# Cluster similarities by float32 matmuls on four column tiles, with the prologue in another order

## The chip, the cores and the metric

The kernel runs on one NeuronCore of a Trainium2 chip. TensorE multiplies matrices and writes to PSUM, VectorE and ScalarE compute and read PSUM, GpSimd computes beside them, and the queue of SyncE (SP) issues most DMA transfers. The metric is the device time of one execution in microseconds, lower is better.

## What is computed

Three layers follow each other: attention within clusters, a mixture of experts that sends every token to one expert, and a last layer. The change lies in the first. Queries and keys get a cluster each, the centroid with the largest cosine similarity; a query sees only the keys of its own cluster.

```python
B, H, S, D = q.shape            # 2, 8, 768, 64; 16 centroids for each head
c_n = centroids / (norm(centroids) + 1e-06)
q_assign = argmax(einsum('bhsd,hcd->bhsc', q_n, c_n))     # k_assign likewise
mask = q_assign[:, :, :, None] == k_assign[:, :, None, :]
scores = where(mask, scale * q @ k.T, -1e9)
attn = softmax(scores)
x = attn @ v                    # then the experts and the last layer
```

The norm of a query or key does not change which centroid is nearest, so the kernel normalises the centroids alone. Two centroids can be close, so the similarities are wanted to float32 accuracy.

## The kernel before

**Stages.** The attention works on eight pairs of heads (two batches, four pairs each). For a pair, `load_qk` brings queries and keys, by dimension (two heads of 64 on 128 partitions, 768 tokens), into the tile `raw`, of which there are two. `a_hi` (L589, ScalarE) rounds them to fp32r, the reduced float32 of the fast matmul, into the tile `w`, and `a_lo` (L595, GpSimd or VectorE) subtracts that from `raw`: the low part. `a_sims` (L610, L613) multiplies tokens by centroids: for every 128 tokens, the high part by the centroids' high and low parts (64 columns: two halves, two heads, 16 clusters), and the low part by the centroids' high part (32 columns). The tokens are the stationary operand, so the result has them on partitions. `a_sims_red` (L620, VectorE) adds the two halves from PSUM into the tile `sim`. `a_argmax` (L653 to L660, VectorE, three steps) makes one-hot rows `ohb`. `a_moves` (L626, SP) copies parts of `w` between partitions by seven DMAs. `a_aux` (L669, L672, L676, L677) turns the one-hot rows by matmul into auxiliary rows of `w`, which carry the mask into the scores' product, by DMA; `a_aux_first` (L685 to L692) does so for the first head of all without DMA, writing straight into `w`.

**The loop.** `x_max` (L751, L753) and `x_max_halves` (L764, L765, L766) take row maxima of masked scores; `x_row` (L773, L774) turns them into another row of `w`. Then a unit is 128 keys of a head: scores (L799, L800) into one of two PSUM tiles, which `x_max_halves` shares, exponentials (L809, ScalarE), their low parts (L823), and the product with the values (L838 to L840) four units later. `v_scale` (L715 to L729) finds a power of two that scales the values.

**Order.** The program order of each engine is the order in which the code issues, and engines wait for each other by semaphores. The prologue runs a list of names, `PRO`, for the first two pairs; each `warm` in it issues as many idle matmuls (L1188) as the next entry of `WARMS` says. Then, during pair p's twelve units, the work of pair p + 2 (names `hi`, `lo`, `sims`, `red`, `moves`, `arg`, `aux`) is issued at the places that `AT` and `AT_PAIR` give in units. `sims0` and `sims1` (queries, keys) are issued in thirds there, with `b` and `c` for the second and third. `load_qk` of pair p + 3 is issued when pair p begins; that of pair 2 is `lqk2` in `PRO`.

Of the kernel before, what the change touches and what calls it, by code (L numbers as in the profile page):

```python
# [28 lines left out]
# places of the windows, by rising load; the first NF32 use plain float32 products  # L29
CAPS = [128, 176, 192, 200, 208, 224, 240, 320]  # L30
# the first window has its expert picked early, and plain float32 products
CAP0 = CAPS[0]
W0_ROWS = [(t, min(128, CAP0 - 128 * t)) for t in range((CAP0 + 127) // 128)]
# query tiles of the last pair that go (and are gated) first
W0_AT = [3,5]
QT = 3
# chunks of an expert's matrices whose low parts are made by GpSimd
# [12 lines left out]
# the places of the operations beside the pairs' products  # L50
# [69 lines left out]
        'sims0b': 2.0003,  # L120
        'sims0c': 2.0006,
        'sims1b': 4.0003,
        'sims1c': 4.233,
# [45 lines left out]
                   'sims0b': 2.4163,  # L169
                   'sims0c': 2.4166,  # L170
                   'sims1b': 5.5923,
                   'sims1c': 5.5926,
# [38 lines left out]
                   'sims0b': 2.5753000000000004,  # L211
                   'sims0c': 2.702,
                   'sims1b': 4.356,
# [27 lines left out]
                   'sims0b': 2.9203,  # L241
                   'sims0c': 2.952,
                   'sims1b': 4.21,
# [3 lines left out]
                   'row00': 9.523,  # L247
                   'sims1c': 5.27},
# [21 lines left out]
                   'sims0b': 2.9203,  # L270
                   'sims0c': 2.9206,
                   'logb': 8.103299999999999,
                   'acc': 8.554,
                   'sims1b': 4.21,
                   'row00': 9.523,
                   'sims1c': 5.27,
# [19 lines left out]
                   'sims0b': 2.7293000000000003,  # L296
                   'sims0c': 2.7296,
# [3 lines left out]
                   'sims1b': 4.21,  # L301
                   'row00': 9.523,
                   'row01': 10.291,
                   'sims1c': 5.27,
# [22 lines left out]
                   'sims0b': 2.126,  # L327
                   'sims0c': 2.7426,
# [4 lines left out]
                   'sims1b': 4.21,  # L333
                   'sims1c': 5.27,
# [26 lines left out]
                   'sims1b': 3.0163,  # L361
                   'sims1c': 3.0166,
# [28 lines left out]
 'WARMS': [8, 8, 0, 7, 0, 9, 4, 3, 4, 3, 0, 0, 0, 0, 0, 0, 0, 0, 0, 0, 0, 0, 0],  # L391
# [14 lines left out]
def body(ctx, tc, i, o):  # L406
# [21 lines left out]

    qT, kT, v = i["qT"], i["kT"], i["v"]

# [1 line left out]
    def load_qk(p, which=(0, 1)):  # L432
        b, hp = PAIRS[p]
        if "raw" not in st[p]:
# [163 lines left out]
    def a_sims(p, qk, t0=0, t1=NT):  # L598
# [5 lines left out]
        if t0 == 0:  # L604
            s["px", qk] = ps_x.tile([128, 512], F32, tag="px", name=f"psim_{p}_{qk}")
# [1265 lines left out]
```

## Time and profile before

| | |
|---|---|
| runs shown | 657.06, 657.48, 664.31 us; median 657.48 |
| span of the profiled execution | 653.1 us |
| TensorE matmuls | 595.3 us busy, 91% of the span, 4814 instructions |
| VectorE | 477.0 us, 73% |
| ScalarE | 318.4 us, 49% |
| GpSimd | 334.3 us, 51% |
| mean granted clock of TensorE | 0.937 of full speed |

The profile has no other time of the profiled execution than its span, from the first to the last instruction. The attention takes it up to 284 us, then come the gating, the experts (303 to 519 us) and the last layer. Busy time of an engine is a sum over its instructions; what it means in a stretch is read from that stretch.

### The profile page before, as it was taken

To read this page: it belongs to the slowest core of one execution; us is meant where nothing else is said; L and a number is where in the kernel's file an instruction comes from. 1 tells how busy PE (TensorE), PEld (TensorE's weight loads), DVE (VectorE), ACT (ScalarE), POOL (GpSimd) and SP (SyncE) were. 2 spreads that over 40 slices of the span, in tenths; PEclk is the share of its full clock that TensorE was granted. 3 is DMA by queue.
4 is the path that set the end of the run, shared out by engine and by line. 5 is a ranking of instruction groups with operands and counts; after the bars stand their busy time and mean duration, and the time that the engine had idled before them with its cause. 6 is when DMAs were issued, how large, how long until landed. Compare 5 with 4: busy or idle time off the path is not lost. (4 is left out here: it accounts for less than half of the span.)

```text
span 653.1 us, 12986 instructions
## 1 busy us (share of the span) xinstructions
PE 595.3 (91%) x4814; PEld 519.0 (79%) x4814; DVE 477.0 (73%) x860; ACT 318.4 (49%) x684; POOL 334.3 (51%) x341
## 2 busy tenths in 40 slices
PE   7989899999899999969898789898799999999996
PEld 4578788888787888859798788786699778888884
DVE  5856788778677877844779999999978766446540
ACT  3334546455445465521576766664566543323230
POOL 6064747455456667532366756767841663333321
PEclk8957899889788999988999999998899999999999
DMA  6853626253612201075477757676670000000001
GB/s 204 223 151 86 181 83 181 84 166 99 185 40 62 51 30 61 24 287 207 159 252 248 248 206 280 225 254 186 153 192 1 3 16 18 16 33 17 32 17 48
DMA packets 28215, 81.80 MB, mean 125 GB/s; under 512 B 4699, under 2 KB 4971, under 8 KB 28146
## 3 DMA queue, kind: packets, MB, share of 16 engines
q1 hardware_dynamic: 22690, 69.30, 34.7%
q0 software_dynamic: 2352, 6.32, 2.6%
q10 hardware_dynamic: 3104, 5.28, 2.5%
q8 instruction: 41, 0.67, 0.4%
q14 instruction: 28, 0.23, 0.1%
HBM read 55.24 MB, written 11.55 MB: 102 GB/s over the span
## 5 line engine op out<-in xcount | busy, mean ns | idle before, releaser
L823 POOL TENSOR_TENSOR pl<-pe 128x768 f16<-128x768 f32 (+1 forms) x90 | 127.3, 1420 | 95.7 <-ACT pe L809 95.5
L1394 POOL TENSOR_TENSOR wk<-rw,wk 128x512 fp32r<-128x512 f32 x67 | 98.6, 1483 | 72.3 <-ACT wk L1393 59.3
L809 ACT ACTIVATE pe<-pS 128x384 f32<-128x384 f32 x192 | 85.1, 488 | 80.2 <-PE pS L800 72.6
L753 DVE TENSOR_REDUCE ohb<-pm 128x1 bf16<-128x768 f32 x84 | 80.1, 954 | 39.8 <-PE pm L751 38.8
L799 PE MATMUL pS<-w 81*128 81x384 f32 x192 | 79.3, 413 | 1.4 <-DVE mh L765 1.3
L1477 PE MATMUL po<-h,wk 128*128 128x352 f32 (+5 forms) x192 | 62.5, 377 | 17.6 <-DVE h L1506 15.4
L800 PE MATMUL pS<-w 128*128 128x384 f32 x192 | 70.1, 365 | 0.0
L838 PE MATMUL pa<-v,pe 128*128 128x65 f16 x576 | 67.2, 200 | 0.0
L1393 ACT ACTIVATE wk<-rw 128x512 fp32r<-128x512 f32 x112 | 65.6, 625 | 2.0 <-DMA rw<-in_w_dram 1.0
L839 PE MATMUL pa<-v,pe 128*128 128x64 f16 x576 | 66.3, 200 | 0.0
L840 PE MATMUL pa<-v,pl 128*128 128x65 f16 x576 | 66.1, 198 | 0.0
L838 PEld LDWEIGHTS <-pe 128*128 128x128 bf16 x576 | 55.2, 102 | 11.1 <-issue 8.5
L1477 PE MATMUL ph<-xTm,wk 128*128 128x352 f32 (+5 forms) x192 | 62.5, 379 | 1.4 <-DVE xTm L1454 1.3
L751 PE MATMUL pm<-w 80*128 80x512 f32 (+1 forms) x168 | 49.5, 379 | 7.5 <-DVE ohb L753 4.5
L839 PEld LDWEIGHTS <-pe 128*128 128x128 bf16 x576 | 55.9, 102 | 0.0
L840 PEld LDWEIGHTS <-pl 128*128 128x128 f16 x576 | 55.8, 102 | 0.0
L1477 PEld LDWEIGHTS po<-h,wk 128*128 128x128 f32 x192 | 36.2, 189 | 21.9 <-ACT wk L1393 8.1
L1478 PE MATMUL po<-h,wk 128*128 128x176 f32 (+5 forms) x192 | 49.7, 259 | 0.0
L1394 DVE TENSOR_TENSOR wk<-rw,wk 128x512 fp32r<-128x512 f32 x45 | 46.4, 1044 | 4.4 <-ACT wk L1393 2.9
L1478 PE MATMUL ph<-xTm,wk 128*128 128x176 f32 (+5 forms) x192 | 49.6, 258 | 0.0
L1731 DVE TENSOR_REDUCE sm<-h 128x1 f32<-128x512 f32 x24 | 15.4, 685 | 43.7 <-PE h L1401 41.2
L1736 ACT ACTIVATE e<-h,sm,smeta 128x512 f32<-128x512 f32 x24 | 18.5, 775 | 56.3 <-DVE sm L1732 56.3
(265 smaller groups left out, 1622.1 us busy)
## 6 DMA issues: line engine op xcount, KB each, us to landing
rw<-in_w_dram SPq DMA_DIRECT2D x56, 512.0 KB
w<-w SPq DMA_DIRECT2D x48, 192.0 KB
xs_d<-zrow ACTq DMA_DIRECT2D x8, 512.0 KB
w_w<-in_w_dram SPq DMA_DIRECT2D x8, 512.0 KB
rw<-in_w_in_dram SPq DMA_DIRECT2D x8, 512.0 KB
rw<-in_w_out_dram SPq DMA_DIRECT2D x8, 512.0 KB
raw<-in_qT_dram SPq DMA_DIRECT2D x8, 384.0 KB
raw<-in_kT_dram SPq DMA_DIRECT2D x8, 384.0 KB
```

The source lines that it names most:

```text
L753: nc.vector.tensor_reduce(out=s["oh"][:, t, 0, h, C : C + 1], in_=pm, op=ALU.max, axis=AX.X)
L799: nc.tensor.matmul(pS, w[0:81, M0 + h, 1, ts], w[0:81, M0 + h, 0, c0:c1], start=b0 == 0, stop=False, skip_group_check=True)
L800: nc.tensor.matmul(pS, w[:, B0 + h, 1, ts], w[:, B0 + h, 0, c0:c1], start=False, stop=True, skip_group_check=True)
L809: nc.scalar.activation(pe[:, e0 - b0 : e0 + n], s["bank"][:, : kb * n], AF.Exp, scale=0.125)
L823: eng.tensor_tensor(out=pl, in0=pe, in1=ph, op=ALU.subtract)
L838: nc.tensor.matmul(pa[:, o0 : o0 + D + 1], ph[:, qs], vh, start=(t == 0 and qt == q0), stop=False, skip_group_check=True)
L839: nc.tensor.matmul(pa[:, o0 : o0 + D], ph[:, qs], vl, start=False, stop=False, skip_group_check=True)
L840: nc.tensor.matmul(pa[:, o0 : o0 + D + 1], pl[:, qs], vh, start=False, stop=(t == NT - 1), skip_group_check=True)
L1393: nc.scalar.activation(t[:, 0, :], rw, AF.Copy)
L1394: (eng or nc.vector).tensor_tensor(out=t[:, 1, :], in0=rw, in1=t[:, 0, :].bitcast(F32), op=ALU.subtract)
L1477: nc.tensor.matmul(out, w[:, 0, ds_], x, start=first, stop=False, skip_group_check=True)
L1478: nc.tensor.matmul(out[:, 0], w[:, 1, ds_], x[:, 0], start=False, stop=last, skip_group_check=True)
```

## The change

The similarity block becomes four plain float32 matmuls. The centroids are now the stationary operand, 32 columns (two heads, 16 clusters, block diagonal), and the tokens as loaded (`raw`) the moving one. Matmul j takes the j-th 32 tokens of every 128, 192 in all, and writes to PSUM partitions 32j to 32j + 31, that is through the j-th quarter of the array's columns. The result has clusters on partitions; one VectorE transpose of 32x32 blocks puts the tokens there and writes `sim`. The centroids need no high and low parts, and `bd` no zero fill on ScalarE (GpSimd fills it). The names `sims0b` to `sims1c` go; a block is issued whole at the place of its first third. The low part of pair 1's queries moves from VectorE to GpSimd, the prologue's list is written anew, and it has 30 warming matmuls instead of 43, none of them in the first pair's units, where 3 stood.

```diff
-    bd = keep.tile([128, NP, 2, 2, C], F32R, name="bd")
+    bd = keep.tile([128, NP, 2, C], F32, name="bd")
+    nc.gpsimd.memset(bd, 0.0)
...
-            nc.scalar.activation(bd[sl, :, 0, r, :], pcv[sl, :, r, :], AF.Copy)
-            nc.vector.tensor_tensor(
-                out=bd[sl, :, 1, r, :], in0=pcv[sl, :, r, :], in1=bd[sl, :, 0, r, :].bitcast(F32), op=ALU.subtract)
+            nc.scalar.activation(bd[sl, :, r, :], pcv[sl, :, r, :], AF.Copy)
...
-    def a_sims(p, qk, t0=0, t1=NT):
+    def a_sims(p, qk):
...
-        for t in range(t0, t1):
-            ts = slice(t * 128, t * 128 + 128)
-            nc.tensor.matmul(
-                px[:, t * 64 : t * 64 + 64], w[:, M0, qk, ts],
-                bd[:, hp].rearrange("p l h c -> p (l h c)"), start=True, stop=False, skip_group_check=True)
-            nc.tensor.matmul(
-                px[:, t * 64 : t * 64 + 32], w[:, lo, qk, ts],
-                bd[:, hp, 0].rearrange("p h c -> p (h c)"), start=False, stop=True, skip_group_check=True)
+        px = s["px", qk] = ps_x.tile([128, 512], F32, tag="px", name=f"psim_{p}_{qk}")
+        toks = s["raw"][:, qk, :].rearrange("p (t j a) -> p j t a", j=4, a=32)
+        for j in range(4):
+            nc.tensor.matmul(px[32 * j : 32 * j + 32, : NT * 32].rearrange("p (t a) -> p t a", a=32),
+                             bd[:, hp].rearrange("p h c -> p (h c)"), toks[:, j], start=True, stop=True)
 
     def a_sims_red(p, qk):
...
-        nc.vector.tensor_reduce(
-            out=s["sim"][:, :, qk], in_=px[:, : NT * 64].rearrange("p (t l c) -> p t c l", t=NT, l=2),
-            op=ALU.add, axis=AX.X)
+        nc.vector.transpose(s["sim"][:, :, qk], s["px", qk][:, : NT * 32].rearrange("p (t c) -> p t c", c=32))
...
-        '1,0': 'v',
+        '1,0': 'p',
...
- 'WARMS': [8, 8, 0, 7, 0, 9, 4, 3, 4, 3, 0, 0, 0, 0, 0, 0, 0, 0, 0, 0, 0, 0, 0],
+ 'WARMS': [8, 7, 5, 2, 2, 2, 2, 2] + [0] * 16,
...
- 'PRO': ['bd0', 'hi00', 'hi01', 'warm', 'cnorm', 'identb', 'lo00', 'csplit', 'hi10', 'lo10', 'lo01', 'hi11', 'warm',
...
+ 'PRO': ['hi00', 'warm', 'cnorm', 'csplit', 'hi01', 'identb', 'sims00', 'red00', 'lo00', 'sims01', 'red01', 'lo01',
+         'moves0', 'warm', 'arg00', 'arg01', 'arg02', 'lv1', 'hi10', 'hi11', 'aux', 'warm', 'x0', 'warm', 'x1', 'arg10',
+         'sims10', 'x2', 'warm', 'lo10', 'red10', 'arg11', 'x3', 'row0', 'sims11', 'warm', 'arg12', 'x4', 'lo11',
+         'red11', 'aux0', 'warm', 'x5', 'vs0', 'moves1', 'aux1', 'lqk2', 'lv2', 'row1', 'vs1', 'vs2', 'vsp0', 'late',
+         'warm']}
```

Lines of the changed kernel have other numbers, since comments went too. Three places show what moved.

TensorE, in the first pair's units, around the similarity block of pair 2's keys (`psim`) behind a halved maximum (`pmh`) and ahead of a count (`pcn`). Before, the two rows of `psim` stand six times:

```order
L751 MATMUL pm_10_570<-w_161 128x256
L764 MATMUL pmh_11_0_575<-w_161 128x384
L764 MATMUL pmh_11_1_578<-w_161 128x384
L610 MATMUL psim_1_582<-bd,w_450 128x64
L613 MATMUL psim_1_582<-bd,w_450 128x32
...
L699 LDWEIGHTS onesb
L699 MATMUL pcn_596<-ohb_149,onesb 128x68
```

And now:

```order
L710 MATMUL pm_10_510<-w_159 128x256
L723 MATMUL pmh_11_0_515<-w_159 128x384
L723 MATMUL pmh_11_1_518<-w_159 128x384
L575 MATMUL psim_1_522<-raw_337,bd 32x192 x4
L658 LDWEIGHTS onesb
L658 MATMUL pcn_528<-ohb_148,onesb 128x68
```

Twelve matmuls that read the split operand `w` have become four that read `raw`; the place is the same.

VectorE, in the prologue: the first head's row maxima (into `ohb`, those in halves through `mh`), the values' maximum (`am`) and the small steps of their scale (`m`, `vsc`). Before, the small steps lie between the first maxima, and `am` was taken earlier still:

```order
L753 TENSOR_REDUCE ohb_147<-pm_0_332 128x1
L765 TENSOR_REDUCE mh_1_343<-pmh_1_0_344 128x1
L765 TENSOR_REDUCE mh_1_343<-pmh_1_1_347 128x1
L766 TENSOR_TENSOR ohb_147<-mh_1_343 128x1
L721 TENSOR_REDUCE m_0_355<-pv_353 1x1
L722 TENSOR_SCALAR m_0_355<-m_0_355 1x1
L723 TENSOR_SCALAR m_0_355<-m_0_355 1x1
L724 TENSOR_SCALAR m_0_355<-m_0_355 1x1
L753 TENSOR_REDUCE ohb_147<-pm_2_360 128x1
L729 COPY vsc_370<-pvb_368 128x1
```

And now, at the end of the maxima:

```order
L712 TENSOR_REDUCE ohb_146<-pm_4_299 128x1
L581 STREAM_TRANSPOSE sim_262<-psim_1_291 128x6x32
L724 TENSOR_REDUCE mh_5_313<-pmh_5_0_314 128x1
L724 TENSOR_REDUCE mh_5_313<-pmh_5_1_317 128x1
L725 TENSOR_TENSOR ohb_146<-mh_5_313 128x1
L674 TENSOR_REDUCE am_321<-vraw_103 128x1
L680 TENSOR_REDUCE m_0_349<-pv_347 1x1
L681 TENSOR_SCALAR m_0_349<-m_0_349 1x1
L682 TENSOR_SCALAR m_0_349<-m_0_349 1x1
L683 TENSOR_SCALAR m_0_349<-m_0_349 1x1
L688 COPY vsc_356<-pvb_354 128x1
```

The scale of the values now stands behind the last of the six maxima, and the second head's argmax steps and the transposes of pair 1 stand between the maxima.

SP, from the moves of pair 0 (the smaller `w`) on: loads of values (`vraw`), the moves of pair 1, the loads of pair 2 (`raw`) and the auxiliary rows of pair 0's second head (`aux`). Before:

```order
L626 DMA w_161<-w_161 64x768 x6
L442 DMA vraw_245<-in_v_dram 128x768
L626 DMA w_188<-w_188 64x1536
L626 DMA w_188<-w_188 64x768 x6
L437 DMA raw_295<-in_qT_dram 128x768
L437 DMA raw_295<-in_kT_dram 128x768
L676 DMA w_161<-aux_325 16x768
L677 DMA w_161<-aux_325 17x768
L442 DMA vraw_351<-in_v_dram 128x768
```

And now:

```order
L585 DMA w_159<-w_159 64x768 x6
L413 DMA vraw_218<-in_v_dram 128x768
L585 DMA w_220<-w_220 64x1536
L585 DMA w_220<-w_220 64x768 x6
L635 DMA w_159<-aux_305 16x768
L636 DMA w_159<-aux_305 17x768
L408 DMA raw_337<-in_qT_dram 128x768
L408 DMA raw_337<-in_kT_dram 128x768
L413 DMA vraw_340<-in_v_dram 128x768
```

The auxiliary rows have passed the loads of pair 2.

## Rows read from the trace of the kernel before

**Rows 1.** Stretches: us, then busy time of PE, PEld, DVE, ACT, POOL; clock, DMA, GB/s

```profile
30.00:57.00 27.00, 24.15 (x135) 20.94 (x135) 16.04 (x36) 11.16 (x21) 13.25 (x10) 0.62 0.57 159
57.00:284.00 227.00, 215.98 (x2646) 189.03 (x2645) 177.97 (x315) 121.50 (x252) 134.19 (x107) 0.92 0.34 96
```

**Rows 2.** Timeline of PE, similarity blocks: start, length, instruction, wait before it and releaser

```profile
39.43 0.26 PE L610 MATMUL psim<-bd,w 128*128 128x64 f32 x1
...
41.85 0.52 PE L699 MATMUL pcn<-ohb,onesb 128*128 128x68 bf16 x6
...
74.74 0.28 PE L613 MATMUL psim<-bd,w 128*128 128x32 f32 x1 [1.03 <-DVE w L595]
...
75.99 0.20 PE L838 MATMUL pa<-v,pe 128*128 128x65 f16 x1
```

**Rows 3.** Timeline of PE, plain float32 products of the first expert window

```profile
305.90 1.06 PE L1475 MATMUL po<-h,w_w 128*128 128x128 f32 x8
306.79 1.06 PE L1475 MATMUL ph<-x2T,w_w 128*128 128x128 f32 x8
```

**Rows 4.** Timeline of DVE in the prologue

```profile
11.24 0.56 DVE L620 TENSOR_REDUCE sim<-psim 128x192 f32<-128x384 f32 x1
...
12.76 0.95 DVE L715 TENSOR_REDUCE am<-vraw 128x1 f32<-128x768 f32 x1 [0.96 <-DMA vraw<-in_v_dram]
...
14.21 0.35 DVE L653 TENSOR_REDUCE mx<-sim 128x12 f32<-128x192 f32 x1
...
22.78 0.96 DVE L753 TENSOR_REDUCE ohb<-pm 128x1 bf16<-128x768 f32 x1 [0.87 <-PE pm L751]
...
24.78 0.27 DVE L721 TENSOR_REDUCE m<-pv 1x1 f32<-1x128 f32 x1
...
26.38 0.14 DVE L729 COPY vsc<-pvb 128x1 f32<-128x1 f32 x1
...
28.54 1.01 DVE L765 TENSOR_REDUCE mh<-pmh 128x1 f32<-128x384 f32 x2
29.59 0.16 DVE L766 TENSOR_TENSOR ohb<-mh 128x1 bf16<-128x1 f32 x1
```

**Rows 5.** Waits of PE from 30 to 284 us: total, times, longest

```profile
PE pm L751 <- DVE ohb L753: 4.1, 7, 1.0
PE pmh L764 <- DMA w<-aux: 3.6, 2, 2.2
...
PE psim L613 <- DVE w L595: 1.6, 2, 1.0
```

**Rows 6.** Timelines of SP's queue, ACT and PE, first 36 us

```profile
1.37 0.45 SPq L437 DMA_DIRECT2D raw<-in_qT_dram  x1
...
4.57 0.84 ACT L589 ACTIVATE w<-raw 128x768 fp32r<-128x768 f32 x1 [2.01 <-DMA raw<-in_qT_dram]
...
15.10 1.10 SPq L626 DMA_DIRECT2D w<-w  x2
...
19.88 0.80 ACT L690 ACTIVATE w<-paux_q 16x768 fp32r<-16x768 f32 x1 [7.99 <-PE paux_q L685]
...
26.86 0.59 SPq L437 DMA_DIRECT2D raw<-in_qT_dram  x1
...
29.96 0.44 PE L799 MATMUL pS<-w 81*128 81x384 f32 x1
...
30.66 0.49 ACT L809 ACTIVATE pe<-pS 128x384 f32<-128x384 f32 x1
...
35.42 0.87 PE L751 MATMUL pm<-w 80*128 80x512 f32 x2 [2.74 <-DMA w<-aux]
```

**Rows 7.** Windows of 4 us: columns as in rows 1, granted clock third from the end

```profile
12.00:16.00 4.00, 4.00 (x16) 3.09 (x17) 3.06 (x7) 0.00 (x0) 4.00 (x8) 0.50 0.41 107
...
36.00:40.00 4.00, 4.00 (x20) 3.75 (x18) 3.64 (x5) 2.05 (x4) 3.31 (x3) 0.50 0.03 10
...
52.00:56.00 4.00, 4.00 (x39) 3.30 (x37) 2.19 (x7) 1.90 (x4) 1.55 (x2) 0.50 0.69 162
```

More of the change, by code (lines that the diff above doesn't have):

```diff
@@ L119 @@
         'l_g0': 11.92,
[L120 to L123, printed above, removed]
         'logb': 8.0003,
@@ L168 @@
                    'row01': 10.105,
[L169 to L172, printed above, removed]
                    'vs1': 2.621,
@@ L246 @@
                    'acc': 8.554,
-                   'row00': 9.523,
-                   'sims1c': 5.27},
+                   'row00': 9.523,},
              '3': {'red0': 3.025,
@@ L326 @@
                    'aux1': 11.775,
-                   'sims0b': 2.126,
-                   'sims0c': 2.7426,
                    'logb': 8.103299999999999,
@@ L332 @@
                    'row00': 9.523,
-                   'sims1b': 4.21,
-                   'sims1c': 5.27,
                    'sims1': 4.116,
@@ L476, in body @@
     nc.vector.memset(warmb, 0.0)
-    zf = keep.tile([128, NP * 64], F32, name="zf")
-    nc.gpsimd.memset(zf, 0.0)
     trib = const.tile([128, 128], BF16, name="trib")
     identb = const.tile([128, 128], BF16, name="identb")
-    bd = keep.tile([128, NP, 2, 2, C], F32R, name="bd")
+    bd = keep.tile([128, NP, 2, C], F32, name="bd")
+    nc.gpsimd.memset(bd, 0.0)
     def cent_norm():
@@ L1121, in body @@
         "lo0": ("a", lambda p: a_lo(p, 0)), "lo1": ("a", lambda p: a_lo(p, 1)),
-        **{f"sims{qk}{k}": ("a", lambda p, qk=qk, t0=t0: a_sims(p, qk, t0, t0 + 2))
-           for qk in range(2) for k, t0 in (("", 0), ("b", 2), ("c", 4))},
+        "sims0": ("a", lambda p: a_sims(p, 0)), "sims1": ("a", lambda p: a_sims(p, 1)),
         "red0": ("a", lambda p: a_sims_red(p, 0)), "red1": ("a", lambda p: a_sims_red(p, 1)),
@@ L1190, in body @@
     PRO = {
-        "bd0": lambda: nc.scalar.activation(bd.rearrange("p a b c d -> p (a b c d)"), zf, AF.Copy),
         "cnorm": cent_norm, "csplit": cent_split, "identb": lambda: nc.vector.tensor_copy(identb, identf),
@@ L1204, in body @@
     }
-    PRO_ORDER = """bd0 warm cnorm hi00 lo00 csplit hi01 identb lo01 warm hi10 lo10 hi11 lo11 sims00 red00 vs0 warm
+    PRO_ORDER = """warm cnorm hi00 lo00 csplit hi01 identb lo01 warm hi10 lo10 hi11 lo11 sims00 red00 vs0 warm
         sims01 red01 moves0 warm sims10 arg00 arg01 arg02 arg10 arg11 arg12 sims11 moves1 warm lv1 lqk2 lv2 aux warm
```

22 lines of the change are left out of this document (removed), and 6 rows, old and new, of tables (AT, PLACES).

## The prediction

> **What bounds the kernel now.** I read the stretches first [rows 1]. From 57 to 284 us, where the attention of the eight pairs of heads runs at pace (twelve units of scores each), TensorE is busy 215.98 of 227 us and VectorE 177.97: work taken from TensorE there comes off the end almost one to one, work taken from VectorE only where TensorE waits for it. From 30 to 57 us, the first pair, TensorE is also busy nearly all the time, but at a granted clock of 0.62. The clock has two levels, 2.4 GHz and half of it; the windows of 4 us [rows 7] show it at half after the first similarity products (12 to 16 us) and again from 36 to 56 us. What went before the second fall is one wait of 2.74 us, at 35.42, for the auxiliary rows of the first pair's second head [rows 6]. The experts and the last layer, after 303 us, are not touched. The waits of TensorE [rows 5] are few: 4.1 us for VectorE's row maxima, 3.6 us for auxiliary rows, and 1.6 us in which a similarity product stood for the low part of its operand.
>
> **The similarity products in the pairs.** There are 16 blocks (8 pairs, queries and keys); the prologue holds 4, the loop 12. A block is now 12 matmuls, each loading a 128x128 weight for 64 or 32 columns. The timeline gives its price [rows 2]: at half clock from 39.43 to 41.85, 2.42 us, and two blocks of the twelve stand in that stretch; at full clock 11 matmuls take 74.74 to 75.99, so 12 take 1.36 us. Together 2 x 2.42 + 10 x 1.36 = 18.4 us of TensorE.
> A new block is four plain float32 matmuls of 32 stationary columns and 192 moving ones, one for each quarter of the array's columns. No row shows such a tile. The nearest rows are the plain float32 products of the first expert window [rows 3]: each is recorded as two passes, and 8 passes of 128 columns take 306.79 - 305.90 = 0.89 us, 0.111 us each, so a pass of 192 columns is 0.167 us. One after the other, the 8 passes of a block are 1.34 us: nothing gained. If all four quarters ran beside each other, a block is 2 passes, 0.33 us. I take the middle: the second pass of a quarter has to follow its first, and the next quarter's first pass may run beside it, so that 5 steps remain, 0.83 us, and 1.67 at half clock. That makes 2 x 1.67 + 10 x 0.83 = 11.6 us, 6.8 saved. TensorE has 11 us of idle time in the stretch, other engines close behind; I count four fifths, **5.5 us**. Bounds: 0 to 11 (of 18.4 - 4.7 = 13.7).
>
> **The low parts.** The new products read the loaded operand itself, no longer the split one. The 1.6 us of waits for the subtraction [rows 5] have nothing left to wait for: **1.6 us**. The loads that free this buffer stand an iteration later, so the longer life of the loaded tile delays none.
>
> **VectorE.** A reduction of 384 values, 0.56 us, gives way to a transpose of 192 from PSUM. No row shows one; a pass over 192 values took 0.35 us [rows 4], over 384 0.56, which are the bounds; by the size I take 0.36. Twelve times 0.2 is 2.4 us, hidden except under the 4.1 us that TensorE waits for maxima: **0.9 us**. Two subtractions on the centroids and a fill by ScalarE go from the prologue, where both engines have slack.
>
> **The prologue, 0.** Its similarity blocks no longer gate anything: VectorE could have the first head's clusters by about 11 us (an estimate: two transposes and five argmax steps). But the auxiliary rows of that head overwrite places that seven SBUF moves read first, and the fifth of these is issued at 15.10 in the kernel before, behind an earlier move that the change leaves where it was. It lands between then and 19.88, when ScalarE wrote those rows; a load of twice its size was used 3.20 us after its issue (1.37 to 4.57), so I take 18.3 [rows 6]. ScalarE's 0.80 us makes it 19.1, and VectorE's first maximum starts some 0.6 later, 19.7 against 22.78. Then VectorE has, by the order shown above, three maxima of 0.96, three in halves of 1.17, five argmax steps of 0.35 and two transposes of 0.36 [rows 4]: 8.9 us, to 28.6 instead of 29.75. Now the scale of the values comes behind them, where before it lay between [rows 4]: its maximum 0.95, then what stood from 24.78 to 26.38, 1.6 us of small steps to and fro between VectorE and TensorE, and two warming matmuls, 0.4, before the scores: they start at about 31.5 against 29.96.
> On SP the auxiliary rows of the second head now stand ahead of the loads of pair 2. So the 2.74 us wait should go: the rows depend on the last maximum (28.6), and with about 1 us for the matmuls and ScalarE and 0.7 for each of two issues (estimates) they leave by 31.0 and land before the second unit wants them (about 33.5). Behind them the loads leave at 31.0 instead of 26.86 and land 3.2 us later, 34.2. ScalarE's split of that operand waits for it, and the second unit's exponentials stand in the same queue behind the split; the halved maximum of that unit needs the PSUM that they free: 34.2 + 0.84 + 2 x 0.49 = 36.0. Before, its first maximum ended at 36.29 [rows 6]. The stall has changed its cause, not its end: **0**, and the bounds are -3 to +6.
>
> **Sum.** 5.5 + 1.6 + 0.9 = 8.0 us off a span of 653.1; the median of the runs shown, 657.48, lies 4.4 above that span, which stays: **649.5 us**.
>
> The Trainium skill, "TensorEngine Tiling (Array Packing)", section Key Properties, says that changing the tiling mode drains TensorE, and that tiles work independently. No run here shows either yet. The first speaks against the change (24 drains in the loop); an estimate from the rows for one, the length of a float32 record less its pitch, about 0.16 us, would take 3.9 us of the gain.
>
> **Rivals.** (a) *The clock stays up in the first pair.* The wait that preceded the fall at 36 us is broken up into smaller ones, and two blocks of small matmuls in that stretch get shorter. For it: the stretch of 20 us at 0.50 follows one gap. Against it: by the working above TensorE idles from about 13 to 19 us in the new prologue, so the clock may be down already, and four units of scores and maxima did not bring it back before. At full clock the 20 us would be 10 by TensorE alone, but VectorE is busy 16.04 of the 27 us; I take 7 us: 642.5. Chance 0.25.
> (b) *The quarters run one after the other, or the switching eats the gain:* 1.34 us a block, no gain on TensorE; 8.0 less 5.5 leaves 2.5: 655. For it: no row shows two matmuls of different columns side by side. Chance 0.20.
> (c) *All four quarters run side by side:* 0.33 us a block, 11 instead of 5.5: 644. Chance 0.12. The Trainium skill, "TensorE: Matmul & The Clock Gate", Part 3, has this as a rule: matmuls on different column tiles run concurrently.
> (d) *Slower: the prologue becomes TensorE's.* If the clock falls in the gap ahead of 19.1 us and the quarters are serial, TensorE has there at half clock six maxima of 768 columns at 0.64, eight warming matmuls of 512 at 0.43, two blocks at 2.7 and 18 small matmuls of 128 at 0.11: 14.7 us against VectorE's 8.9. The scores start 5.8 later and the pairs gain only 2.5: 661. It decides as soon as this work passes 8.9 us, about at two blocks of 1.3 with the clock at half the whole time. Chance 0.08.
>
> **How the numbers follow.** The forecast has 0.35, (a) 0.25, (b) 0.20, (c) 0.12, (d) 0.08. Two per cent, 13.1 us, is about what a measurement of this kernel can tell from no change: under 644.3 is faster, over 670.6 slower. Faster: all of (a) and half of (c), 0.31. Slower: the far end of (d), 0.02. Within: 0.67. The range goes from 639 ((a) with some of (c)) to 661 ((d)); outside it are (a) and (c) in full together, and (d) with a new stall.
>
> **What would show it.** Right: the blocks' four matmuls overlapping in the timeline, 0.8 us a block at full clock; no wait of a similarity product for a low part; transposes near 0.36 us; the first scores at 31 to 32 us; no wait for auxiliary rows at 35 us but one of ScalarE for the loads of pair 2; the half clock between 36 and 56 us as before. Wrong: a block of 1.3 us or of 0.33; a first maximum much before 19 us (then the moves are not what holds it); a granted clock of 1.00 in the first pair; or a new wait in the pairs that is not there now.

## The result, and the profile after

The changed kernel takes 639.32 us (median) against 657.36 of the kernel before, a ratio of 0.974 with an interval of 0.970 to 0.978. The sum had 649.5; the gain is 18 us where I had 8. A ratio, here and below, leaves out executions more than 1.5% above the fastest of their kernel; a median holds them all. The profiled execution spans 636.1 us, 17.0 less than before.

The stretches come first, as in [rows 1]. The pairs' part now ends at 270 instead of 284 us (columns as there: stretch and length, busy time of PE, PEld, DVE, ACT and POOL, granted clock, DMA share, GB/s).

```profile
30.00:57.00 27.00, 23.77 (x132) 17.21 (x133) 18.16 (x38) 12.30 (x23) 14.60 (x11) 0.57 0.57 170
57.00:270.00 213.00, 197.92 (x2618) 167.20 (x2618) 179.25 (x324) 120.09 (x250) 134.32 (x106) 0.98 0.38 108
```

TensorE is busy 18 us less from 57 us on, and its granted clock there is 0.98, not 0.92. The first pair is at half clock as before. Whatever was won lies in the pairs 0 to 5, the ones beside which similarity blocks run: from the second matmul of the first scores to that of the first scores of pair 6 it was 30.2 to 233.8 us, and is 31.5 to 216.9. That is 18.2 us less, while the prologue is 1.3 us longer; pairs 6 and 7 take 25.6 and 21.6 us in both.

A block in the timeline of PE, first at half clock, then at full, each with the matmul behind it (start, length, instruction):

```profile
40.90 0.87 PE L575 MATMUL psim<-raw,bd 128*32 128x192 f32 x8
41.70 0.29 PE L658 MATMUL pcn<-ohb,onesb 128*128 128x68 bf16 x2
...
72.87 0.53 PE L575 MATMUL psim<-raw,bd 128*32 128x192 f32 x8
73.33 0.20 PE L797 MATMUL pa<-v,pe 128*128 128x65 f16 x1
```

Eight passes of 192 columns (four quarters, two passes each) fit into 41.70 - 40.90 = 0.80 us at half clock and 73.33 - 72.87 = 0.46 us at full. Before, the block of [rows 2] took 2.42 and, by the prediction's working, 1.36. One after the other, eight passes would be 1.34 at full clock (the estimate of the prediction): the four quarters do run beside each other.

The similarity tile's instructions by line (shortest, median, longest in ns; first and last start), and the waits of PE from 30 to 270 us (total, times, longest):

```profile
L575 PEld LDWEIGHTS psim<-raw,bd x128: 106/109/173, 6.1 to 198.3; 128*32 128x32 f32 x128
L575 PE MATMUL psim<-raw,bd x128: 322/350/529, 6.2 to 198.4; 128*32 128x192 f32 x128
L581 DVE STREAM_TRANSPOSE sim<-psim x16: 359/373/383, 6.7 to 202.7; 128x192 f32<-128x192 f32 x16
```

```profile
PE pm L710 <- DVE ohb L712: 5.3, 10, 1.0
PE pmh L723 <- DMA w<-aux: 3.6, 2, 2.2
PE pvb L686 <- DVE m L683: 2.1, 3, 1.0
```

The transpose takes 0.37 us. The wait of a similarity product for a low part [rows 5] is gone; the wait for VectorE's maxima has grown from 4.1 to 5.3 us.

The prologue, in the timelines of ACT, DVE and PE (compare [rows 4, 6]):

```profile
16.89 0.80 ACT L649 ACTIVATE w<-paux_q 16x768 fp32r<-16x768 f32 x1 [6.18 <-DMA w<-w]
...
35.96 0.84 ACT L557 ACTIVATE w<-raw 128x768 fp32r<-128x768 f32 x1 [2.74 <-DMA raw<-in_qT_dram]
```

```profile
18.40 0.96 DVE L712 TENSOR_REDUCE ohb<-pm 128x1 bf16<-128x768 f32 x1 [3.33 <-PE pm L710]
```

```profile
30.85 0.88 PE L758 MATMUL pS<-w 81*128 81x384 f32 x1
```

The first head's rows wait for the SBUF moves until 16.89, the first maximum starts at 18.40, the first scores at 30.85, and the stall in the second unit is now ScalarE's wait for the loads of pair 2, 2.74 us up to 35.96 (of TensorE's wait for auxiliary rows there 0.82 us are left). The chain went as I had written it, each link 0.6 to 1.4 us early, the last one 1.8 us late.

### The profile page after: what moved, and what is told of

Its sections match the earlier page's. It is cut to its first block, busy times and chain, and to the rows that moved or that the text cites. A ratio compares the mean times of both kernels' runs of the same rounds, so it can differ in the third digit from the quotient of the medians.

```text
span 636.1 us, 12840 instructions
## 1 busy us (share of the span) xinstructions
PE 571.0 (90%) x4732; PEld 485.9 (76%) x4734; DVE 478.6 (75%) x857; ACT 318.1 (50%) x683; POOL 338.1 (53%) x342
## 5 line engine op out<-in xcount | busy, mean ns | idle before, releaser
L1351 POOL TENSOR_TENSOR wk<-rw,wk 128x512 fp32r<-128x512 f32 x67 | 98.8, 1488 | 66.8 <-ACT wk L1350 54.6
L758 PE MATMUL pS<-w 81*128 81x384 f32 x192 | 76.9, 401 | 3.3 <-DVE mh L724 2.0
L759 PE MATMUL pS<-w 128*128 128x384 f32 x192 | 68.0, 354 | 0.0
L797 PE MATMUL pa<-v,pe 128*128 128x65 f16 x576 | 64.1, 196 | 0.0
L798 PE MATMUL pa<-v,pe 128*128 128x64 f16 x576 | 63.4, 196 | 0.0
L799 PE MATMUL pa<-v,pl 128*128 128x65 f16 x576 | 63.1, 194 | 0.0
L797 PEld LDWEIGHTS <-pe 128*128 128x128 bf16 x576 | 53.4, 99 | 11.7 <-issue 9.4
L798 PEld LDWEIGHTS <-pe 128*128 128x128 bf16 x576 | 54.1, 99 | 0.0
L799 PEld LDWEIGHTS <-pl 128*128 128x128 f16 x576 | 54.0, 100 | 0.0
```

The costliest lines, as they stand in the source:

```text
L758: nc.tensor.matmul(pS, w[0:81, M0 + h, 1, ts], w[0:81, M0 + h, 0, c0:c1], start=b0 == 0, stop=False, skip_group_check=True)
L759: nc.tensor.matmul(pS, w[:, B0 + h, 1, ts], w[:, B0 + h, 0, c0:c1], start=False, stop=True, skip_group_check=True)
L797: nc.tensor.matmul(pa[:, o0 : o0 + D + 1], ph[:, qs], vh, start=(t == 0 and qt == q0), stop=False, skip_group_check=True)
L798: nc.tensor.matmul(pa[:, o0 : o0 + D], ph[:, qs], vl, start=False, stop=False, skip_group_check=True)
L799: nc.tensor.matmul(pa[:, o0 : o0 + D + 1], pl[:, qs], vh, start=False, stop=(t == NT - 1), skip_group_check=True)
L1351: (eng or nc.vector).tensor_tensor(out=t[:, 1, :], in0=rw, in1=t[:, 0, :].bitcast(F32), op=ALU.subtract)
```

## Where the clock came from

The sum held nothing for the clock behind the first pair, and there it differs most. Counted from the granted clock in the trace, pairs 1 to 5 hold 34.1 us at half clock before and 6.8 after; pair 0 holds 20.5 and 21.5. Pairs 3 and 4 show the two effects apart. Windows of before:

```profile
135.50:164.20 28.70, 28.16 (x359) 24.92 (x358) 24.12 (x41) 16.65 (x35) 18.06 (x14) 1.00 0.53 150
164.20:201.30 37.10, 34.15 (x359) 29.77 (x358) 25.34 (x41) 17.57 (x37) 18.51 (x14) 0.82 0.36 99
```

and of after:

```profile
129.50:156.80 27.30, 26.80 (x351) 22.35 (x350) 23.74 (x41) 16.66 (x35) 18.55 (x14) 1.00 0.61 158
156.80:188.00 31.20, 28.27 (x351) 23.42 (x350) 24.70 (x41) 17.52 (x37) 18.55 (x14) 0.95 0.42 117
```

Pair 3 is at full clock in both and gains 1.4 us, from its blocks, one of which had waited for a low part. Pair 4 gains 5.9. In it the same wait stands ahead of the fall in both kernels. The timeline of PE before:

```profile
171.26 0.59 PE L764 MATMUL pmh<-w 80*128 80x384 f32 x2 [2.21 <-DMA w<-aux]
...
172.46 0.40 PE L610 MATMUL psim<-bd,w 128*128 128x64 f32 x1
...
175.02 0.67 PE L799 MATMUL pS<-w 81*128 81x384 f32 x1
```

and its clock in the windows behind that wait:

```profile
172.30:175.70 3.40, 3.40 (x21) 3.40 (x19) 1.69 (x8) 0.00 (x0) 0.00 (x0) 0.50 1.01 230
175.70:179.00 3.30, 3.30 (x27) 2.60 (x27) 0.94 (x2) 1.55 (x3) 1.47 (x1) 0.51 0.43 105
```

After, the timeline and the windows at the same place:

```profile
163.85 0.59 PE L723 MATMUL pmh<-w 80*128 80x384 f32 x2 [2.21 <-DMA w<-aux]
...
165.04 0.53 PE L575 MATMUL psim<-raw,bd 128*32 128x192 f32 x8
...
165.51 0.55 PE L758 MATMUL pS<-w 81*128 81x384 f32 x1
```

```profile
165.80:169.10 3.30, 3.30 (x27) 2.60 (x27) 1.49 (x5) 1.55 (x3) 1.41 (x1) 0.50 0.93 201
169.10:172.50 3.40, 3.40 (x41) 2.51 (x39) 1.93 (x4) 1.91 (x5) 1.52 (x2) 1.00 0.16 47
```

Both fall behind a wait of 2.21 us for auxiliary rows. Before, TensorE then spends 175.02 - 172.46 = 2.56 us on an old block, and the clock is down until 179 (and once more from 192.6 to 199.4 in the same pair); after, the block is over in 0.47 us, and the clock is up again at 169.1. "Busy" is 100% in both. From this came the theories of the experiments: that the old blocks' **kind** (32 or 64 columns behind each full-width weight load) holds the clock down, or that the **time** they take, their **waits**, or the new **order** ahead of the first pair does.

## Experiments

Every kernel is timed beside the kernel before on its chip. The table has its median and that of before; the ratio with its interval where enough executions gave one; and from the one profiled execution the length D of the pairs 0 to 5 (from the second matmul of its first scores to that of pair 6, as above), the time B for which the blocks of the pairs 2 to 7 hold TensorE (start of a block, or of a piece of one, to the start of the next other matmul in the timeline, summed over the loop, with what was added to a block), the half-clock time H within D, and the part of H that lies in the pairs 1 to 5 (pair 0 stands next to the prologue).

| kernel | us | before | ratio | D | B | H | H, pairs 1 to 5 |
|---|---|---|---|---|---|---|---|
| before | 657.4 | | | 203.6 | 21.0 | 54.6 | 34.1 |
| after | 639.3 | 657.4 | 0.974 (0.970 to 0.978) | 185.4 | 6.0 | 28.4 | 6.8 |
| after, once more | 640.5 | 656.5 | 0.979 (0.971 to 0.987) | 182.1 | 6.0 | 21.6 | 3.4 |
| full width | 651.3 | 659.8 | 0.990 (0.986 to 0.995) | 193.3 | 18.3 | 27.3 | 17.1 |
| old order | 642.3 | 659.8 | 0.977 (0.968 to 0.986) | 192.1 | 6.0 | 37.5 | 17.1 |
| old blocks | 668.1 | 659.8 | 1.021 (1.009 to 1.033) | 207.6 | 22.1 | 64.1 | 44.4 |
| tokens stationary | 664.3 | 659.8 | | 204.2 | 20.0 | 57.0 | 37.5 |
| short extra | 666.6 | 659.8 | 1.001 (0.991 to 1.010) | 208.1 | 27.5 | 54.6 | 27.3 |
| short extra, once more | 662.5 | 660.0 | | 198.4 | 24.6 | 27.3 | 17.1 |
| long extra | 654.3 | 659.8 | 0.988 (0.977 to 1.000) | 196.7 | 25.2 | 23.9 | 10.2 |
| long extra, same loads | 668.4 | 660.0 | 1.015 (1.007 to 1.023) | 205.5 | 36.6 | 17.1 | 3.4 |
| wait for low parts | 644.7 | 659.8 | | 188.7 | 8.1 | 27.3 | 13.7 |
| early side work | 648.1 | 659.8 | 0.979 (0.968 to 0.990) | 191.1 | 6.0 | 34.1 | 27.3 |
| blocks twice | 642.2 | 656.5 | 0.976 (0.970 to 0.982) | 186.0 | 10.1 | 23.9 | 13.7 |
| extra on one tile | 651.3 | 656.5 | 0.987 (0.979 to 0.995) | 194.1 | 23.6 | 25.6 | 13.7 |
| fill waits | 640.2 | 656.5 | 0.975 (0.969 to 0.982) | 182.7 | 5.7 | 19.5 | 6.8 |
| before + long extra | 664.7 | 655.7 | 1.011 (1.004 to 1.019) | 208.7 | 38.1 | 23.9 | 13.7 |
| rows before loads | 639.8 | 655.7 | 0.973 (0.965 to 0.981) | 182.4 | 6.2 | 17.1 | 3.4 |
| + splits later | 637.5 | 655.7 | 0.970 (0.964 to 0.976) | 182.9 | 5.7 | 13.7 | 6.8 |
| + filling | 639.6 | 655.7 | 0.973 (0.967 to 0.979) | 190.4 | 6.0 | 23.9 | 13.7 |

A least-squares line through these twenty rows is D = 174.5 + 0.66 B + 0.29 H, with 2.2 us left over per row. It is a description, not a proof; the single experiments carry the causes. Two things limit it. One execution of a kernel can differ much from the next: the same kernel has H 54.6 and 27.3 in the two rows of short extra. And behind the last scores of pair 7, where no kernel here is changed, the profiled executions took from 371.9 us (after; before 372.1) to 381.0 (tokens stationary), so that some us between two medians can come from there. D leaves that part out.

**Are the quarters beside each other, and is that worth the time?** Full width:

```
-  nc.tensor.matmul(px[32*j : 32*j+32, :192], bd (32 columns), toks[:, j], start=True, stop=True)
+  nc.tensor.matmul(px[:, :192], bd (128 columns, centroids at 32j), toks[:, j], start=j == 0, stop=j == 3)
```

> The changed kernel with its column tiles undone: every quarter multiplies with a stationary operand of full width (128 columns, the 32 centroids at 32j and zeros beside them), and the four products of 192 columns accumulate over all 128 rows of the result, so that they can only go one after the other. Same result, same order, same waits, same transpose. Theory 1 (the quarters lie beside each other, and that is the larger part of the term that I had too small): the block's first start to last end goes from the 0.80 us that it takes at half clock, and about 0.40 at full, to 2.6 and 1.33, that is + 0.93 in each of ten blocks and + 1.8 in each of two: 9.3 + 3.6 = 13 us, of which four fifths show as in my sum: 639.3 + 10 = 649 to 652 us. Theory 2 (the gain came from the missing waits for low parts and from the order before the first pair, not from the time of the matmuls): 641 to 643 us. Half clock in the pairs 1 to 5: were the clock brought down by time that TensorE spends elsewhere, it would come back from 6.8 us towards the 34 of the kernel before; if the old blocks' kind (small products behind a wait) did that, it stays below 12, since these products are long and dense.

The timeline of PE has the block from 103.74 to 104.91, 1.17 us, between the matmul ahead of it and the next one:

```profile
103.64 0.27 PE L678 MATMUL pv<-cst,am 128*1 128x128 f32 x1
103.74 1.47 PE L575 MATMUL psim<-raw,bd 128*128 128x192 f32 x8
104.91 0.47 PE L758 MATMUL pS<-w 81*128 81x384 f32 x1
```

651.3 us, 12 above after, as theory 1 had it. Between the two profiled executions it is 17.0, of which D has 7.9 and the part behind the pairs 7.4. The blocks take nearly as much TensorE time as the old ones took (B 18.3 against 21.0), without their low parts and their short products, and still a part of the gain stays: two fifths by the ratios, 10.3 of the 18.2 us by D. H is 27.3, as after, but 17.1 of it lie in the pairs 1 to 5, neither under 12 nor near 34: by its place the half clock speaks for neither theory.

> The changed kernel with four further products behind each of the twelve blocks of the pairs 2 to 7: the same quarters once more on the four column tiles, result unread. If the quarters of a block lie beside each other, a block keeps TensorE for 0.39 us more at full clock and 0.73 at half, 10 x 0.39 + 2 x 0.73 = 5.4 us in all, and the time goes up by 4 to 6 us. If the quarters went one after the other in part, as I had it (0.83 and 1.67), 12 us more.

> The same four further products, all sent to the first column tile (each over the result of the one before, unread): same operands, same width, same number of columns, but they can't lie beside each other. If tiles lying beside each other is what makes a block short: 4 x 0.32 = 1.3 us more per block at full clock and 2.6 at half, 10 x 1.3 + 2 x 2.6 = 18 us in all, the time 14 to 18 us above the changed kernel. If narrow stationary operands are quick by themselves: no more than with the four tiles, 4 to 6 us.

```
+  if p >= 2: the four matmuls again, to px[32*j : 32*j+32, 256:448]     # twice
+  if p >= 2: the four matmuls again, to px[0:32, 256:448]               # on one tile
```

The timelines of PE, twice and then on one tile:

```profile
102.99 0.27 PE L682 MATMUL pv<-cst,am 128*1 128x128 f32 x1
103.19 0.53 PE L575 MATMUL psim<-raw,bd 128*32 128x192 f32 x8
103.54 0.51 PE L579 MATMUL psim<-raw,bd 128*32 128x192 f32 x8
103.98 0.45 PE L762 MATMUL pS<-w 81*128 81x384 f32 x1
```

```profile
106.64 0.53 PE L575 MATMUL psim<-raw,bd 128*32 128x192 f32 x8
106.99 1.46 PE L579 MATMUL psim<-raw,bd 128*32 128x192 f32 x8
108.38 0.44 PE L762 MATMUL pS<-w 81*128 81x384 f32 x1
```

Two blocks take 103.98 - 103.19 = 0.79 us where one takes 0.46: the second adds 0.33, exactly the two passes that remain when four quarters lie beside each other. On one tile the same four products add 108.38 - 106.64 - 0.46 = 1.28, eight passes. The change of tiling behind the first block can cost no more than its 0.13 over 0.33. The change ahead of it lies before the block's start, and so outside B: the product for `pv` starts 103.19 - 102.99 = 0.20 us ahead of the block here, and 103.74 - 103.64 = 0.10 ahead of the full-width one. Together that is about 0.2 us a block, 2 to 3 us in twelve. In time the one adds 1.7 us to the median of after on the same chip (less than the 4 to 6 expected), the other 10.8 (14 to 18 expected) for 23.6 - 6.0 = 17.6 us more of B: a microsecond of TensorE in the blocks is worth 0.61 at the end there, not four fifths.

**Blocks or order?**

```
-  'PRO': ['hi00', 'warm', 'cnorm', 'csplit', ...   (new)
+  'PRO': ['hi00', 'hi01', 'warm', 'cnorm', ...     (as before, without 'bd0'); 'WARMS' and '1,0' as before
```

> The new blocks and their transposes with the order ahead of the first pair, the numbers of warming matmuls and the engine of one low part as they were before. Theory 1 (the blocks made the gain, inside the pairs 0 to 5): 638 to 643 us, the pairs 1 to 5 as after within 3 us and at most 12 us of them at half clock. Theory 2 (the new order ahead of the first pair shifted the pairs against what makes the clock fall, or freed the first pairs of a wait): about half of the 18 us is lost, 645 to 650 us, and more than 20 us of half clock in the pairs 1 to 5.

> The old blocks (twelve split products each) and the old reduction, in the new order ahead of the first pair; only the low parts of the first two pairs stand ahead of the blocks that read them. Theory 1 (the blocks made the gain): 655 to 664 us, no better than before, with 25 to 40 us of half clock in the pairs 1 to 5. Theory 2 (the order did): 645 to 650 us with under 15 us of half clock there.

The new blocks in the old order: 642.3 us, ratio 0.977. The old blocks in the new order: 668.1, slower than before, and above the 655 to 664 expected. So the blocks made the gain and the order gave none of it that these runs can tell. The side signs were off in both: 17.1 us of half clock in the pairs 1 to 5 in the one (at most 12 expected), 44.4 in the other (25 to 40). Old blocks need the low parts ahead of them, which the new order puts later; that may be why they do worse in it, with H at 64.1.

**Kind, time or wait?** Tokens stationary, no column tiles, no low parts:

```
+  for t in range(6): nc.tensor.matmul(px[:, 32*t : 32*t+32], raw[:, qk, 128*t : 128*t+128], bd, ...)
+  nc.vector.tensor_copy(sim, px)                # in place of the transpose
```

> The changed kernel with plain float32 products as it has them, but the tokens stationary as they were before: six matmuls of 32 columns in a block, no column tiles, and in place of the block transpose a plain copy of the same 192 columns. It has neither the wait for low parts nor the twelve split products, and its order is the new one; only the block's time differs from after. How long six such matmuls with their float32 weight loads take stands in no row; between the 0.40 us of the new block and the 1.36 of the old one at full clock. Theory 1 (the time of the blocks counts, nearly one for one): 639.3 + 10 to 12 times what the block takes over 0.40, so 645 us for a block of 0.9 and 650 for one of 1.36. Theory 2 (the waits and the order count): 639 to 642 us whatever the block takes.

664.3 us. The windows view over D, first of this kernel, then of the full-width one:

```profile
37.50:241.70 204.20, 192.81 (x2060) 166.80 (x2059) 151.12 (x259) 103.98 (x210) 115.10 (x81) 0.86 0.41 114
```

```profile
33.30:226.60 193.30, 179.31 (x2012) 154.16 (x2011) 153.17 (x260) 103.31 (x211) 115.01 (x81) 0.93 0.44 121
```

Same order, no wait for low parts in either, blocks of 20.0 and 18.3 us in all: the one with short products has a clock of 0.86, the one with long products 0.93. Theory 2 (waits and order alone) falls, since no execution is under 653.2 us. The median is more than theory 1 (the blocks' time alone) allowed, and D grew by 18.8 us for 14.0 more in B; but the executions go from 653.2 to 671.6 us, the profiled one is the longest, and the shortest is no more than after and those 14.0 us. The clock is firmer: 0.912 to 0.936 over the whole span in these four, 0.949 to 0.962 in the ten of full width. Then both kinds were added, unread, behind the new blocks:

```
+  if p >= 2: six matmuls, 128 tokens stationary, 32 columns           # short extra
+  if p >= 2: four matmuls, full width, 192 columns                    # long extra
+  if p >= 2: the six matmuls with 224 columns instead of 32           # long extra, same loads
```

> The changed kernel, with work added behind each of the twelve blocks of the pairs 2 to 7, whose result nobody reads: six float32 products with 128 tokens stationary and 32 columns (the kind of the old blocks, without their waits). In the kernel with the tokens stationary such a block kept TensorE for 1.1 us at full clock and 2.2 at half. Theory 1 (short products on full-width operands bring the clock down, beside the time that they take): 13 to 15 us for the added time and 5 to 8 more for the clock, 639 + 18 to 23 = 657 to 662 us, mean granted clock 0.94 or lower. Theory 2 (the clock falls where TensorE has less to do or other work shifts, whatever the kind of products): 651 to 655 us with a clock of 0.95 to 0.96, as with long extra products.

> The same with added work of the other kind: four float32 products of 192 columns at full width behind each of the twelve blocks, unread as well. In the full-width kernel such a block kept TensorE for 1.1 us at full clock and 2.1 at half, as long as the six short ones. Theory 1 (kind): the added time alone, 639 + 12 to 14 = 651 to 653 us, mean granted clock 0.95 to 0.96, and 5 to 8 us faster than the kernel with short extra products. Theory 2 (time alone): equal to it within 2 us.

> The kernel with six short extra products behind each of twelve blocks once more, beside the long ones on one chip: 662 to 668 us with a mean clock of 0.92 to 0.935.

> The kernel with six short extra products behind each of twelve blocks (tokens stationary, 32 columns), with the same six operands loaded and 224 columns sent past each of them instead of 32, result unread. By the 1.14 us that eight records of 192 columns take, the extra products take about 2.0 to 2.3 us a block instead of 1.35, so TensorE does some 9 to 12 us more work. Theory 1 (the clock falls behind short products, where TensorE mostly loads weights): mean clock 0.95 to 0.96, and the time no more than that of the short ones, 656 to 664 us, in spite of the greater work. Theory 2 (float32 loads of 128 tokens as such, or the added time as such, bring it down): mean clock 0.93 or lower, and 5 to 9 us above the short ones, 670 us or more.

Short and long extra cost TensorE about the same (B 27.5 and 25.2), and end at 666.6 and 654.3; their ratios, 1.001 and 0.988, have intervals that overlap, so it is the clock more than the time that tells them apart. But the short ones don't act in every execution: these fall into two groups, one of 655 to 657 us with a mean clock of 0.954 to 0.956 and one of 664 to 674 us with 0.918 to 0.934; on the first chip the second group is much the larger, on the other chip they are alike. With the clock up they cost no more than the long ones (647 to 659 us, 0.951 to 0.964). The long products behind the same weight loads gave 668.4 us, neither below the short ones nor with a clock of 0.95 in every execution (0.941 to 0.960), so neither theory's numbers hold there; the loads alone don't bring 0.93, and more can't be read from it.

The turned question is the clearest. Long products behind the old short blocks of the kernel before:

```
+  if t1 == NT and p >= 2:
+      for k in range(6): nc.tensor.matmul(px[:, 384:512], raw[:, qk, 128*k : 128*k+128], raw[:, qk, 0:128], ...)
```

> The kernel before, with six float32 products of 128 columns at full width behind the last piece of each of the twelve blocks of the pairs 2 to 7, result unread: about 1.1 to 1.3 us more per block at full clock, twice that at half, 14 to 18 us of TensorE in all. Over the runs so far the time of the pairs 0 to 5 goes up by some 0.66 us for each us that the blocks keep TensorE and 0.34 for each us at half clock. If the old short products bring the clock down for what stands around them too thinly, long products right behind them mend it: half clock in the pairs 0 to 5 from 55 us down to 25 to 35, and 657 to 663 us, about the time of before. If the clock falls for another reason (the time TensorE spends, the waits for low parts), half clock stays at 50 us or more and the time is 666 to 671 us.

The windows view over D, of before and of this kernel:

```profile
30.30:233.90 203.60, 191.28 (x2063) 166.77 (x2062) 151.52 (x260) 104.33 (x211) 114.82 (x81) 0.87 0.41 113
```

```profile
30.20:238.90 208.70, 195.51 (x2207) 172.18 (x2206) 153.58 (x260) 103.68 (x211) 114.30 (x81) 0.94 0.41 110
```

TensorE was given 17 us more to do in the same order with much the same waits (1.0 us for low parts instead of 1.6), and its clock rose from 0.87 to 0.94. The mean clock of the whole span was 0.952 to 0.957 in every execution, against 0.925 to 0.940 of before beside it. So neither TensorE's time nor its waits by themselves hold the clock down there: long products behind the short ones bring it up, while short ones behind the new blocks (short extra) left it at 0.934 or lower in eleven executions of fourteen. Whether it is their shortness or the order around them that lowers it, this run doesn't part. The time was 664.7 us, 9 above before, where this theory had 657 to 663. Of the 10.4 us between the two profiled executions D has 5.1 and the part behind the pairs 5.6: the clock gave back a part of the 17 us, less than I had put on it.

```
+  if p >= 2: nc.tensor.matmul(px[0:32, 256:288], 32 columns, low part of raw[:, qk, :32], ...)   # unread
```

> The changed kernel, with one small product (32 columns, result unread) ahead of each of the twelve blocks of the pairs 2 to 7 that reads the low part which the old blocks read: the old wait alone, without the old products. If the wait's term in my sum (1.6 us) is right: 640 to 642 us, with waits of TensorE for the low parts of 2 to 4 us over the pairs. If the missing wait is what kept the clock up: 645 us or more with a mean clock below 0.945.

In the waits of PE the wait is there again, 1.2 us where before had 1.6:

```profile
PE psim L577 <- DVE w L565: 1.2, 2, 1.0
```

The median of 644.7 lies between the two expectations, with executions from 633.5 to 648.3. That the wait costs something is likely; how much stays open.

**The first pair.** Attempts at keeping its clock up, with the kernel after once more beside the second:

```
-  ..., 'arg02', 'lv1', 'hi10', 'hi11', 'aux', 'warm', 'x0', 'warm', 'x1', 'arg10', 'sims10', ...
+  ..., 'arg02', 'vs0', 'lv1', 'lqk2', 'hi10', 'hi11', 'aux', 'sims10', 'red10', 'sims11', 'red11', 'arg10', 'arg11', 'arg12',
+       'vs1', 'vs2', 'vsp0', 'aux0', 'aux1', 'lo10', 'lo11', 'moves1', 'warm', 'x0', ...      # early side work
-  'WARMS': [8, 7, 5, 2, 2, 2, 2, 2]
+  'WARMS': [8, 20, 20, 2, 2, 2, 4, 6]                                                       # fill waits
```

> An attempt at a faster kernel: the changed one, where the similarity of pair 1, the scales of its values, its moves and the additional rows of pair 0 stand ahead of the row maxima of pair 0 instead of among and behind them, with 10 warming matmuls in the place where TensorE would otherwise wait for them. If the wait for these rows (0.8 and 3.6 us before the first pair's scores) and the side work in the first pair are what holds up its start: first scores at 28 to 31 us and 632 to 638 us in all. If the row maxima (VectorE) are what the first scores wait for, they start as much later as the side work takes, 33 to 35 us, and the time is 639 to 643 us.

> An attempt at a faster kernel: the changed one with the waits of TensorE ahead of the first scores (3.1 us for the first indicator, 2.0 for the first rows of queries, 1.0, 0.5 and 1.0 before the values' scale) filled with warming matmuls: 20, 20, 4 and 6 where it has 7, 5, 2 and 2. If the clock then stays up, the half-clock time ahead of and in the first pair goes from 10 and 21.5 us to under 10 together, and the time to 628 to 635 us; if TensorE falls behind by the added products, the first scores come 1 to 3 us later and the time is 639 to 643 us.

> The changed kernel once more, beside the next three on one chip: 637 to 643 us with a mean clock of 0.95 to 0.96; half clock in the pairs 1 to 5 of the profiled run anywhere between 5 and 20 us.

The side work moved ahead of the maxima took the half clock of pair 0 from 21.5 to 6.8 us, but the scores started at 32.5 and the pairs 2 to 4 had 27.3 us of half clock: 648.1, above both expectations. These are the new blocks, without short products; the kind of the products is not all that the clock in the pairs hangs on. Filling TensorE's waits lowered H to 19.5 (21.6 in after beside it) and started the pair at 33.4 (32.8): 640.2, equal to after.

In the old order with the new blocks the scores had started at 26.5 at full clock, and then TensorE stood 6.4 us for auxiliary rows that were sent behind the loads of pair 2: those of pair 0's second head (the text below calls them pair 1's). Sending them ahead:

```
-  'arg12', 'lqk2', 'aux', 'warm', 'aux0', 'red11', 'x0', 'aux1', 'x1',
+  'arg12', 'aux', 'warm', 'aux0', 'red11', 'x0', 'aux1', 'lqk2', 'x1',            # rows before loads
-  pair 0: 'hi0': 0.541, 'lo0': 1.248
+  pair 0: 'hi0': 2.2, 'hi1': 2.3, 'lo0': 2.25                                     # + splits later
-  'WARMS': [8, 8, 0, 7, 0, 9, 4, 3, 4, 3, 0, 0, 0, ...
+  'WARMS': [8, 8, 0, 7, 0, 9, 4, 3, 4, 3, 4, 6, 4, ...                            # + filling
```

> The new blocks with the old order ahead of the first pair (scores from 26.2 us, at full clock), where one thing is moved: the additional rows of pair 1 are sent ahead of the loads of pair 2 instead of behind them. With the loads ahead TensorE waited 6.4 us for these rows inside the first pair, and its clock fell just there and stayed down for 20 us. If the rows' place behind the loads is what makes them late: that wait falls to under 3 us, half clock in the first pair to 14 us or less, and the time to 632 to 638 us. If the rows are late for another reason (the moves ahead of them), nothing changes: 638 to 643 us.

> The same, and ScalarE's two splits of pair 2 stand behind the third unit of scores instead of among the first two, since ScalarE waited 2.6 us there for their loads, and the exponentials stood behind them. If that wait matters once the rows come earlier: 1 to 3 us below the kernel with the rows alone. If not, within 2 us of it.

> The same, with 4, 6 and 4 warming matmuls beside the first three units of the first pair. If what is left of the wait still brings the clock down, they keep it up: half clock in the first pair under 7 us and 628 to 634 us. If the wait is gone without them, they cost what they take, 1 to 3 us.

The waits of PE, in the old order and with the rows ahead:

```profile
PE pm L710 <- DMA w<-aux: 6.4, 1, 6.4
```

```profile
PE pm L710 <- DMA w<-aux: 2.4, 1, 2.4
```

The wait shrank as expected and the half clock of pair 0 fell from 20.5 to 13.7 us. With the splits later it was 6.8, though the wait was 4.0 us again, so the length of this wait alone does not set it. The times, 639.8 (632 to 638 expected) and 637.5 us, are not below the kernel after by more than the intervals: the scores now start at 29.6 instead of 26.5. Warming matmuls on top gave nothing.

## Why the prediction was wrong in size

**What bounds the kernel** held: work taken from TensorE in the pairs came off the end, and between these two profiles pairs 6 and 7 and all behind them did not move, and the prologue only by 1.3 us.

**The blocks: the step that failed.** I saw that nothing was to be gained with the quarters one after the other (1.34 us) and that all side by side made 0.33, and took the middle, 0.83, for want of a row. The chip does 0.46, of which 0.33 is the two passes: the bound I had given as rival (c) at 0.12. By my own working the blocks take 2 x 0.80 + 10 x 0.46 = 6.2 us of TensorE instead of 11.6, and save 12.2 instead of 6.8. The Trainium skill has this as a rule in "TensorE: Matmul & The Clock Gate", Part 3 (column tiles run concurrently), and these runs agree, with 0.33 us for a second block on four tiles against 1.28 on one. What I set against it were the drains that the Trainium skill, "TensorEngine Tiling (Array Packing)", Key Properties, has for a change of tiling mode. Here the two changes cost about 0.2 us a block, 2 to 3 us in twelve blocks, where I had estimated 3.9. My four fifths were a little high, two thirds by the line through the runs: 12.2 x 0.66 = 8.0 us instead of 5.5.

**The low parts** (1.6) and **the transpose** (0.36 us forecast, 0.37 measured): the wait is gone, and the transposes are as short as I had them. Nothing shows their 0.9 us: TensorE's wait for maxima, out of which it was to come, is 5.3 us instead of 4.1. In B the vanished waits and the pieces of the split blocks are another 15.0 - 12.2 = 2.8 us, by the line 1.8.

**The clock behind the first pair: the term that was missing.** I treated the half clock as a matter of the first pair, though [rows 1] show 0.92 from 57 us on, which is 2 x 0.08 x 227 = 36 us of half clock. 27 of these went with the old blocks. By the line that is 26.2 x 0.29 = 7.7 us over the pairs 0 to 5; together 8.0 + 1.8 + 7.7 = 17.5 of the 18.2 measured. How firm the 7.7 are: B and H are fitted together, and the kernel before with long products gave back less than the line says (D 2.2 us above it). What the experiments show is that kind of product and clock go together, not that the kind alone sets it (early side work has 27.3 us of half clock in the pairs 1 to 5, without a short product); what else does stays open, and the share of the clock in the 18 us is a description with that uncertainty.

**The prologue** was right in its links and in its sum (0 forecast, + 1.3 measured): the stall at 35 us changed its cause and not its end, and rival (a), the clock of the first pair, fell, 20.5 us of half clock before and 21.5 after. But the fall of the clock no longer follows the stall: after, it is 0.99 from 26.0 to 29.2 us, in which TensorE is busy 1.37 us, and 0.50 from 29.2 on, ahead of the first scores. What it fell behind lies in the prologue, as the prediction held against (a), though later than the gap from 13 to 19 us that it named. Rival (b) fell with the overlap, and (d) with it.

## What to carry to other kernels

Matmuls of 32 stationary columns that go to four column tiles cost here what one of them costs, and about 0.2 us for the changes of tiling around them; turning an operand so that this is possible paid here even though another engine has to transpose the result. Where short products on full-width weights stand near TensorE's waits, look at the granted clock of every stretch, not of the worst one alone, and count the half-clock time there as part of what they cost. A moved wait is not a removed one: ask what the same engine will wait for next, and whether its clock falls there again.

## What the runs showed of the hardware that I had not expected

TensorE "busy" is no guard for its clock: in the window from 172.3 to 175.7 us before, it is busy 3.40 of 3.40 us at 0.50. More work raised it: 17 us of long unread products in the kernel before brought the pairs' clock from 0.87 to 0.94. And the same short products, in the same kernel, went with a mean clock of 0.954 to 0.956 in three executions and 0.918 to 0.934 in eleven; why it differs from one execution to the next stays open. The two changes of tiling around a block on column tiles cost about 0.2 us, one ahead of its first matmul and one behind its last.
